# Sixteen stores of rounded weight halves: issued from SyncE's queue or from ScalarE's queue

## The chip, the cores and the metric

The kernel runs on one core of a Trainium2 chip. The metric is the device time of one execution in microseconds (us). Of the kernel before the change there are three timed runs, with a median of 845.52 us (844.38 to 846.73), and one profiled execution, which took 844.22 us and whose profile spans 842.3 us from the first to the last instruction.

## The reference

The work is one attention-like layer followed by a two-layer mixing block, for batch 8, 8 heads, sequence 576 and head size 64 (so the model width is 512 and the hidden width 2048):

```python
kv = np.einsum('bhsd,bhse->bhde', k, v)
out = np.einsum('bhsd,bhde->bhse', q, kv)
rms = np.sqrt(np.mean(out * out, axis=-1, keepdims=True) + 1e-06)
attn = out / rms * g_norm
x = attn.transpose(0, 2, 1, 3).reshape(8, 576, 512)
h = x.transpose(0, 2, 1) @ U @ V            # low rank over the sequence: 576 -> 32 -> 576
u = x + h.transpose(0, 2, 1)
ch = np.maximum(u @ w_ch1, 0.0) @ w_ch2     # 512 -> 2048 -> 512
return u + ch
```

## The kernel before, in words

The two large products, `u @ w_ch1` and the one with `w_ch2`, make up most of the work. TensorE multiplies in a reduced format (`F32R`). To keep float accuracy every operand is split in two: `hi` is the value rounded to `F32R` by a ScalarE cast, and `lo` is the rest, `value - hi`, made by VectorE (`split`, line 143). Each product is then three matmuls: hi by hi, hi by lo, lo by hi.

The 4608 rows of the activation are cut into nine blocks of 512. The first three blocks (`j` = 0, 1, 2; the loop on line 834) are multiplied in the plain way: for each of 16 slices of the hidden width come 12 matmuls of the first layer (`ffn1`, line 511), a rectification with a split on ScalarE (line 524) and VectorE (line 525), and 12 matmuls of the second layer (`ffn2`, line 527). The other six blocks are multiplied in pairs by a scheme of the Strassen-Winograd kind with seven products in place of eight (the loop on line 889). It needs, beside the weights themselves, four sums and differences of the quarters of each weight matrix (`S1` to `S4`). These are the "weight forms".

The forms are made once, during the blocks 1 and 2, by `sums_of_w` (line 259), which is called for 16 pieces: two matrices by eight slices. Each piece has two steps:

- `one` adds the weight halves back together (line 268, two VectorE instructions) and forms the four combinations in place (line 273, four VectorE instructions), in a tile `dec` of 128 by 1024 floats. There are two such tiles, used in turn.
- `two` casts the result to `hi` in the tile `wf` on ScalarE (line 145), subtracts on VectorE so that `dec` holds `lo` (line 146), and stores both to DRAM, as pieces of `w1s` or `w2s`, 512 KB each. There is one `wf` tile (`bufs=1`), so the next piece's cast must wait until the store of `hi` has read `wf`.

The list `PREP` (line 59) gives the place of each piece in the traced order. At the same time the attention of the following batch elements goes on: loads of `kv_sb` and `q_sb`, small matmuls into the banks `pp`, a normalization (lines 358 to 393), a transposition through DRAM (`turn_step`, line 408: stores and loads named `xt`, `ut`), and mixing (`mix_step`, line 496). All its ScalarE and VectorE work shares the two engines with the forms.

Nearly every transfer is issued by SyncE (the rows `SPq`) through the helper `dma` on line 106. One store, on line 662 at the very end, is issued by ScalarE (`ACTq`). Every engine runs its instructions in a fixed order. Which order that is, is settled when the program is built: a planner walks through the traced instructions with a simulated clock and a model of their durations (`schedule_with_timeline_sim=True`, line 961) and puts on each engine what is ready in that simulation. Only instructions given to `keep_in_program_order` are pinned among themselves: nearly all matmuls from line 837 on, the two VectorE additions of line 268, some loads of raw weights and the copies of whole weights to DRAM. The two stores of `two` are not pinned.

Of the kernel before, what the change touches and what calls it, by code (L numbers as in the profile page):

```python
# [10 lines left out]
F32 = mybir.dt.float32  # L11
# [57 lines left out]
def build(ctx: ExitStack, tc: tile.TileContext, kv0_in, kv_in, q_in, uv_in, w_in, out):  # L69
    nc = tc.nc  # L70
# [35 lines left out]
    def dma(out, in_, keep=False):  # L106
        ins = nc.sync.dma_start(out=out, in_=in_)
        if keep:
            tc.keep_in_program_order(ins)
# [5 lines left out]
    def dec_tile(n):  # L115
        return const.tile([P, 2 * DM], F32, name=f"dec{n}", tag=f"dec{n}")
# [26 lines left out]
    def split(hi, lo, src, lo_eng):  # L143

        nc.scalar.copy(out=hi, in_=src)  # L145
        lo_eng.tensor_tensor(out=lo, in0=src, in1=hi.bitcast(F32), op=ALU.subtract)  # L146
# [66 lines left out]
    def halves(t):  # L213
        return t.rearrange("p (a c) -> p a c", a=2)
# [38 lines left out]
    def parts_of_w(which, n):  # L253
        w = "w1 w2".split().index(which)
        return [whole[which, 0] if f == 0 else whole[f][:, 2 * w:2 * w + 2] for f in (n, n + HALF)]
# [3 lines left out]
    def sums_of_w(which, n):  # L259

        c = DM // 2
        t = {}

        def one():
            t["plain"] = a = dec_tile(sets[0] % 2)
            sets[0] += 1
            for k, w in enumerate(parts_of_w(which, n)):
                ins = nc.vector.tensor_tensor(out=halves(a[:, k * DM:(k + 1) * DM]), in0=w[:, :, 0].bitcast(F32), in1=w[:, :, 1].bitcast(F32), op=ALU.add)  # L268
                tc.keep_in_program_order(ins)
            a11, a12, a21, a22 = (a[:, k * c:(k + 1) * c] for k in ((0, 1, 2, 3) if which == "w1" else (0, 2, 1, 3)))  # L270
            for o, in0, in1, op in ((a22, a21, a22, ALU.add), (a21, a11, a21, ALU.subtract), (a11, a22, a11, ALU.subtract),
                                    (a12, a12, a11, ALU.subtract)):
                nc.vector.tensor_tensor(out=o, in0=in0, in1=in1, op=op)  # L273

        def two():
            hi = wf.tile([P, 2 * DM], F32R, name="wf")
            lo = t["plain"].bitcast(F32R)
            split(hi, lo, t["plain"], nc.vector)
            d = dram.tile([P, 4, 2, c], F32, name=f"{which}s{n}")
            for s, part in enumerate((hi, lo)):  # L280
                dma(d[:, :, s], part.bitcast(F32).rearrange("p (a c) -> p a c", a=4))
            for k, name in enumerate(("S2", "S4", "S3", "S1") if which == "w1" else ("S2", "S3", "S4", "S1")):
                wd[which, n, name] = d[:, k]

        return [one, two]
# [684 lines left out]
```

## Time and profile before

| what | value |
|---|---|
| median of three runs | 845.52 us (844.38 to 846.73) |
| profiled execution, its own time | 844.22 us |
| span of its profile | 842.3 us |
| TensorE (PE) busy | 831.6 us, 99% of the span |
| VectorE (DVE) busy | 605.4 us, 72% |
| ScalarE (ACT) busy | 380.0 us, 45% |
| first cast to `wf` for a form / last one | starts at 155.6 / 300.1 us |
| stores of `hi` | 16 of 512 KB, issued by SyncE |
| granted TensorE clock | 1.000 throughout |

A matmul's end is modelled in the profile and matmuls overlap, so the busy time says when TensorE had something running, not how well it ran. What counts for this kernel is the idle time before TensorE's instructions, and what ended it. An idle time of another engine only matters if TensorE ends up waiting behind it.

### The profile page before, as it was taken

How to read it: one execution, taken by the hardware profiler on the slowest of the kernel's cores; microseconds unless marked ns; L12 is line 12 of the kernel's file. 1: busy time of each engine (PE TensorE's matmuls, PEld its weight loads, DVE VectorE, ACT ScalarE, POOL GpSimd, SP SyncE). 2: the span in 40 equal slices, each digit the busy share in tenths (PEclk: the TensorE clock that was granted, in tenths of full speed). 3: DMA queues.
4: the chain of work that ended last, by engine and by line, in shares of the span. 5: the costliest groups of instructions: out<-in, count | busy, mean ns of one | idle time of the engine just before them, and what ended most of it. 6: DMA issues, size and time to landing. Idle time of an engine off the chain costs nothing.

```text
span 842.3 us, 12663 instructions
## 1 busy us (share of the span) xinstructions
PE 831.6 (99%) x4581; PEld 694.3 (82%) x4581; DVE 605.4 (72%) x991; ACT 380.0 (45%) x663; POOL 8.3 (1%) x37
## 2 busy tenths in 40 slices
PE   8999999999999999999999999999999999999998
PEld 8888888888887888888888878888888888888886
DVE  4788655778898877767957898568667965762574
ACT  4766422333244444465436653644355444332431
POOL 3000000000000000000000000000000000000000
PEclk9999999999999999999999999999999999999999
DMA  9996975666487764577878678866765786666665
GB/s 339 385 375 227 370 261 213 237 202 196 139 288 255 222 182 139 162 239 240 258 226 285 208 227 253 273 212 193 228 206 174 224 268 204 184 187 211 193 202 175
DMA packets 105229, 195.00 MB, mean 232 GB/s; under 512 B 10320, under 2 KB 41296, under 8 KB 101456
## 3 DMA queue, kind: packets, MB, share of 16 engines
q1 hardware_dynamic: 105024, 194.07, 70.4%
q8 instruction: 37, 0.61, 0.3%
q14 instruction: 24, 0.20, 0.1%
q10 hardware_dynamic: 144, 0.13, 0.0%
HBM read 142.91 MB, written 51.25 MB: 231 GB/s over the span
## 4 chain that ended last, share of the span: by engine, by line
PE 89%; DVE 5%; DMA 4%; ACT 1%; issue 1%; SPq 0%; DVEq 0%; ACTq 0%
PE y L102 67%; PE h L102 13%; PE pp L102 9%; DMA w2s<-dec 1%; DMA kvq<-kv_in 1%; DMA w2s<-wf 1%; DMA w1s<-wf 1%; DVE dec L268 1%; DVE ss L369 1%; DVE hhl L525 1%; DVE dec L273 1%; ACT wf L145 1%; DMA ringw<-w2s 1%; DVE dec L146 0%; DVE dec L133 0%
## 5 line engine op out<-in xcount | busy, mean ns | idle before, releaser
L102 PE MATMUL y<-entry,ring 128*128 128x512 f32 x576 | 136.0, 390 | 0.0
L102 PE MATMUL y<-hhl,ws 128*128 128x512 f32 x540 | 132.3, 392 | 0.0
L102 PEld LDWEIGHTS y<-entry,ring 128*128 128x128 f32 x576 | 107.5, 188 | 22.2
L102 PE MATMUL h<-uth,ws 128*128 128x512 f32 x360 | 120.4, 395 | 1.4 <-ACT uth L155 0.7
L102 PEld LDWEIGHTS y<-hhl,ws 128*128 128x128 f32 x540 | 99.9, 188 | 20.1
L594 DVE TENSOR_TENSOR h<-y,h 128x512 f32<-128x512 f32 x71 | 48.6, 689 | 57.4 <-PE y L102 52.1
L102 PE MATMUL y<-uB,ringw 128*128 128x512 f32 x354 | 85.0, 391 | 0.0
L638 DVE TENSOR_TENSOR entry<-h,entry 128x1024 fp32r<-128x1024 f32 x48 | 58.6, 1220 | 35.0 <-ACT entry L637 34.8
L102 PE MATMUL y<-uT,ring 128*128 128x512 f32 x348 | 82.4, 390 | 0.0
L102 PEld LDWEIGHTS h<-uth,ws 128*128 128x128 f32 x360 | 67.5, 188 | 16.6 <-DVE hhl L525 1.7
L102 PEld LDWEIGHTS y<-uB,ringw 128*128 128x128 f32 x354 | 66.0, 188 | 13.6
L102 PEld LDWEIGHTS y<-uT,ring 128*128 128x128 f32 x348 | 65.0, 188 | 13.6 <-ACT h L601 0.2
L637 ACT CAST entry<-h 128x1024 fp32r<-128x1024 f32 x48 | 50.5, 1052 | 44.7 <-PE y L102 44.2
L102 PE MATMUL h<-utl,ws 128*128 128x512 f32 x180 | 70.3, 391 | 0.0
L524 ACT ACTIVATE hhl<-h 128x512 fp32r<-128x512 f32 x47 | 28.0, 596 | 76.4 <-PE h L102 76.3
L102 PE MATMUL y<-hhl,ringw 128*128 128x512 f32 x216 | 55.2, 390 | 0.5 <-DMA ringw<-w2s 0.5
L102 PE MATMUL y<-entry,ringw 128*128 128x512 f32 x216 | 55.1, 390 | 0.0
L102 PE MATMUL y<-uT,ringw 128*128 128x512 f32 x210 | 51.0, 391 | 0.0
L102 PEld LDWEIGHTS y<-hhl,ringw 128*128 128x128 f32 x216 | 40.4, 188 | 9.5 <-DMA ringw<-w2s 0.9
L102 PEld LDWEIGHTS y<-entry,ringw 128*128 128x128 f32 x216 | 40.3, 188 | 8.3
L525 DVE SCALAR_TENSOR_TENSOR hhl<-h,hhl 128x512 fp32r<-128x512 f32 x47 | 32.1, 682 | 20.5 <-ACT hhl L524 20.3
L102 PEld LDWEIGHTS y<-uT,ringw 128*128 128x128 f32 x210 | 39.1, 188 | 8.2 <-issue 0.2
(200 smaller groups left out, 1185.9 us busy)
## 6 DMA issues: line engine op xcount, KB each, us to landing
ring<-wd SPq DMA_DIRECT2D x69, 256.0 KB, 3.9
kv_sb<-kv_in SPq DMA_DIRECT2D x14, 1216.0 KB, 7.8
ringw<-wd SPq DMA_DIRECT2D x66, 256.0 KB, 3.7
wd<-ws SPq DMA_DIRECT2D x15, 1024.0 KB, 8.7
raw<-w_in SPq DMA_DIRECT2D x30, 511.8 KB, 10.2
ring<-w1s SPq DMA_DIRECT2D x48, 256.0 KB, 3.6
ringw<-w1s SPq DMA_DIRECT2D x48, 256.0 KB, 3.6
ring<-w2s SPq DMA_DIRECT2D x48, 256.0 KB, 3.7
```

The source lines that it names most:

```text
L102: ins = nc.tensor.matmul(*args, **kw)
L145: nc.scalar.copy(out=hi, in_=src)
L268: ins = nc.vector.tensor_tensor(out=halves(a[:, k * DM:(k + 1) * DM]), in0=w[:, :, 0].bitcast(F32), in1=w[:, :, 1].bitcast(F32), op=ALU.add)
L273: nc.vector.tensor_tensor(out=o, in0=in0, in1=in1, op=op)
L369: nc.vector.tensor_reduce(out=ss.rearrange("p (i h) -> p i h", h=2), in_=xv, axis=AX.X, op=ALU.add)
L524: nc.scalar.activation(out=hh, in_=h, func=AF.Relu)
L525: nc.vector.scalar_tensor_tensor(out=hl, in0=h, scalar=0.0, in1=hh.bitcast(F32), op0=ALU.max, op1=ALU.subtract)
L594: nc.vector.tensor_tensor(out=out, in0=in0, in1=in1, op=ALU.add)
L637: nc.scalar.copy(out=hi, in_=src)
L638: nc.vector.tensor_tensor(out=lo, in0=src, in1=hi.bitcast(F32), op=ALU.subtract)
```

## The change

The store of `hi` is issued by ScalarE on its own queue, where before SyncE issued it. The store of `lo` stays with SyncE. Sizes, destinations and data are the same.

```diff
             lo = t["plain"].bitcast(F32R)
             split(hi, lo, t["plain"], nc.vector)
             d = dram.tile([P, 4, 2, c], F32, name=f"{which}s{n}")
-            for s, part in enumerate((hi, lo)):
-                dma(d[:, :, s], part.bitcast(F32).rearrange("p (a c) -> p a c", a=4))
+            for s, (part, queue) in enumerate(((hi, nc.scalar), (lo, nc.sync))):
+                queue.dma_start(out=d[:, :, s], in_=part.bitcast(F32).rearrange("p (a c) -> p a c", a=4))
             for k, name in enumerate(("S2", "S4", "S3", "S1") if which == "w1" else ("S2", "S3", "S4", "S1")):
                 wd[which, n, name] = d[:, k]
```

## The prediction

> **What bounds the kernel now.** I began with the page, then split the span at the first cast into `wf`, at the last store of a form, and where the tail begins, and read TensorE's idle time in each piece.
>
> ```profile
> span 842.3 us, 12663 instructions
> PE 831.6 (99%) x4581; PEld 694.3 (82%) x4581; DVE 605.4 (72%) x991; ACT 380.0 (45%) x663; POOL 8.3 (1%) x37
> ```
> ```profile
> core 0: us, PE busy (x) PEld busy (x) DVE busy (x) ACT busy (x) POOL busy (x), PEclk, DMA share, GB/s
> 0.00:155.60 155.60, 151.72 (x953) 128.53 (x954) 101.61 (x182) 75.89 (x141) 8.33 (x37) 1.00 0.82 310
> 155.60:302.40 146.80, 144.00 (x897) 119.98 (x896) 124.41 (x250) 58.98 (x118) 0.00 (x0) 1.00 0.66 210
> 302.40:640.00 337.60, 337.12 (x1859) 281.48 (x1858) 251.86 (x414) 167.10 (x301) 0.00 (x0) 1.00 0.71 222
> 640.00:842.30 202.30, 198.73 (x877) 164.28 (x875) 127.53 (x150) 78.07 (x104) 0.00 (x0) 1.00 0.65 203
> ```
>
> TensorE is idle for 842.3 - 831.6 = 10.7 us in all. Of that 155.60 - 151.72 = 3.88 us lie before the first moved store, and 3.57 us in the tail, far behind the last one. The stage that the change touches (155.6 to 302.4 us) has 146.80 - 144.00 = 2.80 us of idle TensorE. So even a perfect change to this stage is worth 2.8 us, about 0.33%. In the stage VectorE is busy for 124.41 of 146.80 us (85%) and ScalarE for 58.98 us (40%): VectorE is the tight helper, ScalarE has room on the average. The clock column stays at 1.00, so it plays no part.
>
> TensorE's own waits in 150 to 300 us, and ScalarE's group of the 16 casts:
>
> ```profile
> PE pp L102 <- DVE x L391: 1.0, 1, 1.0
> PE pp L102 <- DVE st L165: 0.8, 2, 0.5
> PE y L102 <- DVE st L538: 0.6, 1, 0.6
> PE h L102 <- DVE hhl L525: 0.3, 1, 0.3
> ```
> ```profile
> L145 ACT CAST wf<-dec 128x1024 fp32r<-128x1024 f32 x16 | 16.8, 1049 | 16.0 <-DVE dec L273 6.3 <-DMA w1s<-wf 5.6 <-DMA w2s<-wf 4.0
> ```
>
> All of TensorE's waits here end on VectorE. ScalarE sat idle for 5.6 + 4.0 = 9.6 us before its casts because the previous store of `hi` had not yet left `wf`. The question is how much of these 9.6 us reaches TensorE through VectorE, and whether the new queue shortens them.
>
> **The change, part by part.**
>
> *SyncE loses 16 issues.* These are the stores themselves, and how long SyncE waited for the casts:
>
> ```profile
> L107 SPq DMA_DIRECT2D w1s<-wf x8: 513/522/603, 156.7 to 271.0; - x8
> L107 SPq DMA_DIRECT2D w2s<-wf x8: 513/524/712, 168.2 to 301.2; - x8
> DMA to landing us min/median/max: 3.2/4.2/10.1
> ```
> ```profile
> SPq L107 <- ACT wf L145: 17.7, 8, 3.7
> ```
>
> That is 16 x 0.52 = 8.4 us of issue time and 17.7 us of waiting. But the next thing of this piece on SyncE is the store of `lo`, which needs the subtraction behind the same cast, so SyncE mostly waits there instead. None of TensorE's waits above names a transfer. I count this part at nothing. What covers it is that SyncE's loads are wanted well after they are issued. Without that cover it would be worth at most the stage's 2.80 us.
>
> *ScalarE gains 16 issues.* Each waits for its own cast to end, and what stands behind it on ScalarE waits too. The trace has one store issued by ScalarE, of 128 KB; beside it is SyncE's own row for the same line, and the slowest comparable issue on SyncE:
>
> ```profile
> L662 ACTq DMA_DIRECT2D out<-st x1: 374/374/374, 839.6 to 839.6; - x1
> L662 SPq DMA_DIRECT2D out<-st x24: 332/338/405, 494.3 to 839.2; - x24
> L107 SPq DMA_DIRECT2D w2s<-dec x8: 513/682/1329, 169.4 to 302.4; - x8
> ```
>
> ScalarE's 374 ns lie within SyncE's 332 to 405 ns, so I take SyncE's 0.52 us for the 512 KB store; the bounds are 0.37 and 1.33 us. Also lost is the overlap with the next instruction. The places with a late TensorE behind them decide. The first is the cast at 188.18 us, with all its followers up to TensorE's 0.31 us wait:
>
> ```profile
> 178.84 1.05 ACT L145 CAST wf<-dec 128x1024 fp32r<-128x1024 f32 x1 [0.63 <-DVE dec L273]
> 179.01 0.35 SPq L107 DMA_DIRECT2D kv_sb<-kv_in  x1
> 179.92 0.71 SPq L107 DMA_DIRECT2D w2s<-wf  x1
> 184.73 0.60 ACT L524 ACTIVATE hhl<-h 128x512 fp32r<-128x512 f32 x1 [4.41 <-PE h L102]
> 188.18 1.05 ACT L145 CAST wf<-dec 128x1024 fp32r<-128x1024 f32 x1 [2.85 <-DMA w2s<-wf]
> 189.13 0.61 ACT L466 ACTIVATE uth<-ut,g_sb 128x384 fp32r<-128x384 f32 x1
> 189.26 1.22 DVE L146 TENSOR_TENSOR dec<-dec,wf 128x1024 fp32r<-128x1024 f32 x1 [3.04 <-ACT wf L145]
> 190.13 0.26 ACT L359 ACTIVATE x<-pp 64x128 f32<-64x128 f32 x1
> 190.93 0.81 DVE L369 TENSOR_REDUCE ss<-x 128x10 f32<-128x640 f32 x1
> 193.86 0.67 DVE L525 SCALAR_TENSOR_TENSOR hhl<-h,hhl 128x512 fp32r<-128x512 f32 x1
> 194.59 0.50 PE L102 MATMUL h<-uth,ws 128*128 128x512 f32 x1 [0.31 <-DVE hhl L525]
> ```
>
> The cast ends at 189.23; with 0.03 us to release the store (179.92 against the end at 178.84 + 1.05 = 179.89) and 0.52 us of issue, the next activation starts at about 189.78 in place of 189.13, 0.65 us later. Line 359 then ends at 190.13 + 0.26 + 0.65 = 191.04, and the reduction that needs it started at 190.93: 0.1 us late. The rest is hidden behind VectorE's own queue. The second place:
>
> ```profile
> 231.86 0.36 SPq L107 DMA_DIRECT2D kv_sb<-kv_in  x1
> 233.50 0.52 SPq L107 DMA_DIRECT2D w1s<-wf  x1
> 239.69 1.05 ACT L145 CAST wf<-dec 128x1024 fp32r<-128x1024 f32 x1 [4.29 <-DMA w1s<-wf]
> 240.65 0.59 ACT L524 ACTIVATE hhl<-h 128x512 fp32r<-128x512 f32 x1
> 241.92 0.68 DVE L525 SCALAR_TENSOR_TENSOR hhl<-h,hhl 128x512 fp32r<-128x512 f32 x1
> 243.99 0.97 PE L102 MATMUL y<-hhl,w2s 128*128 128x512 f32 x3 [0.58 <-DVE st L538]
> ```
>
> Here the activation at 240.65 would end at 240.65 + 0.59 + 0.65 = 241.89, and VectorE took it up at 241.92: just hidden. So ScalarE's 16 issues cost about +0.1 us. At 1.33 us an issue they add 0.81 us at each of the two places, 1.7 us in all; at 0.37 us they cost nothing. I take +0.1.
>
> *The store of `hi` no longer queues behind SyncE's loads.* It leaves no earlier: on SyncE it already left 0.03 us after the cast. But at both places above a load of `kv_sb` (1216 KB) had been issued 0.91 and 1.64 us before on the same queue, and the chain of waits shows what the stores then took:
>
> ```profile
> 179.92 8.16 DMA w2s<-wf
> 233.50 6.09 DMA w1s<-wf
> 255.70 8.92 DMA w2s<-dec
> ```
>
> 8.16 and 6.09 us against a median of 4.2. At the median the casts could go at 185.33 (after the activation of 184.73) and about 237.7, which is 2.8 and 1.9 us earlier; VectorE's idle 3.04 us before line 146 shrinks alike, and TensorE's 0.31 and 0.58 us go: -0.9 us. If the store shares the DMA engines evenly with the load, it still lands later than 4.2 us. Bounds: -0.9 us and 0. I take -0.6, nearer to the first, since half of the gain in landing already covers the 0.31 and most of the 0.58. The third row is a store of `lo`, which stays on SyncE behind another such load; it leads to the waits on lines 391 and 165 (1.8 us), which stay.
>
> [...]
>
> **Sum.** +0.1 - 0.6 + 0 = -0.5 us on the profiled execution's 844.22 us (span 842.3 and 1.9 around it). That execution lies 1.3 us below the median of the runs; carried to the median, 845.52 - 0.5 = 845.0 us. The known unknowns reach from -0.9 to +1.8 us, 844.6 to 847.3. A change of less than 0.3% (2.5 us) can't be told from none.
>
> **The rivals.**
>
> *The store lands no sooner.* Sixteen engines move the same bytes, and the load is ahead with its packets; then only ScalarE's +0.1 us is left: 845.6 us. [...] Against it: nothing in the trace, but 8.16 against 4.2 us looks like waiting in a line. Chance 0.24.
>
> *The planner writes another order.* The two stores aren't pinned, and a different simulated time on ScalarE and SyncE can put other VectorE instructions first, with VectorE 85% busy. Favourably, all 2.8 us of idle TensorE in the stage go: 842.7 us. Unfavourably, as much is added: 848.3 us. For it: all four of TensorE's waits end on VectorE. Against it: the matmuls are pinned, and most late VectorE instructions have slack. Chance 0.26, evenly over that span, so about 0.05 on either side beyond 2.5 us.
>
> *The store stands behind a waiting activation.* Then the change does not do what it says: "behind the cast" holds in the traced order only. If the planner sets a rectification between cast and store, the store waits for TensorE first.
>
> ```profile
> L524 ACT ACTIVATE hhl<-h 128x512 fp32r<-128x512 f32 x21 | 12.5, 596 | 34.5 <-PE h L102 34.4
> ```
>
> The mean idle time before one is 34.5 / 21 = 1.64 us; with its 0.60 us the store leaves 2.2 us late (after the cast at 178.84 it would be 5.4 us, the activation ending at 185.33). `wf` comes free that much later, the next cast and line 146 with it, and at the two places without slack TensorE waits 2 x 2.2 = 4.5 us: 850.0 us, slower. It decides once the store is over 1.3 us late at both places. Against it: SyncE's stores left right after their casts in the same kind of plan. Chance 0.14.
>
> **How the numbers follow.** The forecast, 845.0 us, has 0.36. Slower by over 0.3%: nearly all of the third rival (0.11), 0.05 of the reordering, and 0.03 for a dear issue, 0.19. Faster by over 0.3%: 0.05 of the reordering and 0.02 for scatter, 0.07. No change: 0.74. The range from 843.2 to 848.6 leaves out the best reorderings (0.04) and the third rival with the worst reorderings (0.15).
>
> **What would show it.** Right: ScalarE shows 16 stores of about 0.5 us, each directly behind its cast; `wf` stores behind a `kv_sb` load land in 4 to 6 us; ScalarE's 9.6 us of idle before the casts fall below 5; idle TensorE from 155 to 302 us stays between 1.5 and 3.5 us. Wrong: the landings stay at 6 to 8 us (first rival); TensorE waits for other VectorE lines (second); activations stand between cast and store (third); or TensorE's idle time changes outside this stage, where I expect none.

## The result

| kernel | median | lowest to highest | executions |
|---|---|---|---|
| before | 844.38 us | 842.60 to 846.73 | 7 |
| after | 849.35 us | 847.99 to 853.24 | 7 |

The ratio after to before is 1.0068, with a 95% interval of 1.0054 to 1.0082: the change costs 5.0 us by the two medians and 5.7 us by the ratio, where 845.0 us and no measurable difference had been forecast, and the result lies above the range. The profiled executions took 844.22 us before and 848.63 us after, a difference of 4.4 us.

The head of the page of the kernel after, and its row for the stage that holds the change (same columns as the table of stretches in the prediction):

```profile
span 846.8 us, 12666 instructions
PE 832.6 (98%) x4581; PEld 695.2 (82%) x4581; DVE 605.9 (72%) x991; ACT 380.4 (45%) x663; POOL 8.3 (1%) x37
```
```profile
155.60:302.40 146.80, 142.09 (x844) 118.64 (x843) 122.17 (x244) 56.06 (x110) 0.00 (x0) 0.98 0.65 205
```

TensorE's idle time in the stage rose from 2.80 to 146.80 - 142.09 = 4.71 us, and the granted clock of the stage is now below 1.00, at 0.98. So part of the loss is idle time, and another part is busy time that became longer.

To see where the loss lies, I took instructions that stand in the same place in both kernels as marks. The first is the cast that starts at 178.84 us before; the timeline after has it so:

```profile
179.61 1.05 ACT L145 CAST wf<-dec 128x1024 fp32r<-128x1024 f32 x1 [0.63 <-DVE dec L273]
```

The other two are TensorE's: a second-layer group (256.20 us before, 255.59 after) and a first-layer group (284.04 before, 288.37 after). TensorE in the stretches between the marks, before and then after (columns: us, PE busy and its records, granted clock, DMA share, GB/s):

```profile
core 0: us, PE busy (x), PEclk, DMA share, GB/s
256.20:284.04 27.84, 25.93 (x170) 1.00 0.79 253
155.60:256.20 100.60, 99.72 (x591) 1.00 0.63 204
284.04:842.30 558.26, 554.21 (x2871) 1.00 0.69 213
```
```profile
255.59:288.37 32.78, 28.07 (x170) 0.90 0.67 211
155.60:255.59 99.99, 99.99 (x594) 1.00 0.64 208
288.37:846.80 558.43, 554.39 (x2871) 1.00 0.68 213
```

At the first mark the kernel after is 0.77 us late; that comes from the start, where two profiles of one kernel differ as well (TensorE idle for 5.45 us before 155.60 us in this profile after and for 4.52 us in a second one). From the first mark to the second it gains 1.38 us (0.77 late becomes 0.61 ahead); some half of that is scatter, since a second profile of the kernel before (the eighth experiment) passes this stretch in 76.67 us where the first took 77.36. Between the second and the third, over the same 170 records, it loses 32.78 - 27.84 = 4.94 us. Behind them it loses 0.17 us. The sum, 0.77 - 1.38 + 4.94 + 0.17 = 4.50 us, is the difference of the spans (846.8 - 842.3). So the whole loss of this pair of profiles sits in some 30 us. Of the 4.94 us, 2.80 are added idle time (4.71 against 1.91) and 2.14 are longer busy time (28.07 against 25.93) at the lower clock.

What happened there is seen in the timeline. Before:

```profile
252.62 1.04 ACT L145 CAST wf<-dec 128x1024 fp32r<-128x1024 f32 x1
253.21 0.38 SPq L107 DMA_DIRECT2D q_sb<-q_in  x1
253.68 0.53 SPq L107 DMA_DIRECT2D w2s<-wf  x1
254.30 0.58 SPq L107 DMA_DIRECT2D kv_sb<-kv_in  x1
258.18 1.05 ACT L145 CAST wf<-dec 128x1024 fp32r<-128x1024 f32 x1 [1.18 <-DMA w2s<-wf]
263.33 1.33 PE L102 MATMUL pp<-kvb,q_sb 128*128 128x128 f32 x10
```

After:

```profile
252.85 0.33 SPq L107 DMA_DIRECT2D kv_sb<-kv_in  x1
253.67 1.05 ACT L145 CAST wf<-dec 128x1024 fp32r<-128x1024 f32 x1
254.76 0.52 ACTq L281 DMA_DIRECT2D w2s<-wf  x1
...
264.03 1.04 ACT L145 CAST wf<-dec 128x1024 fp32r<-128x1024 f32 x1 [7.64 <-DMA w2s<-wf]
264.98 0.72 ACT L153 CAST xh<-x 128x640 fp32r<-128x640 f32 x1
265.75 0.69 PE L102 MATMUL pp<-xh,u 128*64 128x128 f32 x4 [3.61 <-ACT xh L153]
267.91 2.44 PE L102 MATMUL pp<-kvb,q_sb 128*128 128x128 f32 x10
```

Before, the load of `kv_sb` (1216 KB) stood behind the store of `hi` (sixth slice of the second matrix) in SyncE's order: the store went as the cast ended, at 253.66 us, and the load 0.62 us behind it. SyncE hardly waited for the cast here (its issue ahead of the store ended at 253.21 + 0.38 = 253.59); what held the load back was its place. After, the store is no longer ahead of it, and the load goes at 252.85. The store also leaves later, because the planner put the cast behind a few small ScalarE instructions (it starts at 253.67 where it started at 252.62). So the load is 1.91 us ahead of the store, and the store, on its own queue, lands late:

```profile
254.76 9.19 DMA w2s<-wf
```

Before it had landed within 4.4 us. `wf` is a single tile, so the next cast waits 7.64 us at the head of ScalarE. Behind that cast, in ScalarE's fixed order, stands the cast of `x` to `xh`, and TensorE waits 3.61 us for it. During this wait, at 264.3 us, the clock falls (TensorE in stretches of 2 us, columns as above):

```profile
264.00:266.00 2.00, 0.25 (x2) 0.58 0.02 5
266.00:268.00 2.00, 1.39 (x10) 0.50 0.87 291
...
270.00:272.00 2.00, 2.00 (x8) 0.72 0.27 41
```

The ten matmuls `pp<-kvb,q_sb` take 2.44 us at a clock of 0.50 where they took 1.33 us.

The rest of the change went as its description says. All 16 stores are on ScalarE's queue (the row has the eight of `w2s`, with the shortest, median and longest issue in ns; those of `w1s` have the same median), and ScalarE's casts waited for 9.9 us on VectorE and 8.8 us on stores:

```profile
L281 ACTq DMA_DIRECT2D w2s<-wf x8: 520/521/539, 168.6 to 305.5; - x8
```
```profile
L145 ACT CAST wf<-dec 128x1024 fp32r<-128x1024 f32 x16 | 16.8, 1050 | 18.7 <-DVE dec L273 9.9 <-DMA w2s<-wf 8.8
```

### The profile page after: what moved, and what is told of

It reads as the page before. It is cut to its first block, busy times and chain, and to the rows that moved or that the text cites. A ratio compares the mean times of both kernels' runs of the same rounds, so it can differ in the third digit from the quotient of the medians.

```text
span 846.8 us, 12666 instructions
## 1 busy us (share of the span) xinstructions
PE 832.6 (98%) x4581; PEld 695.2 (82%) x4581; DVE 605.9 (72%) x991; ACT 380.4 (45%) x663; POOL 8.3 (1%) x37
## 4 chain that ended last, share of the span: by engine, by line
PE 92%; DMA 5%; DVE 1%; ACT 1%; issue 0%; DVEq 0%; SPq 0%; ACTq 0%
PE y L102 68%; PE h L102 14%; PE pp L102 10%; DMA kv_sb<-kv_in 1%; DMA kvq<-q_in 1%; DMA w2s<-wf 1%; DMA raw<-w_in 1%; DMA uvs<-uv_in 1%; DVE dec L133 0%; ACT wf L145 0%; DVE st L165 0%; DVE hhl L525 0%; DVE ws L146 0%; DVE dec L146 0%; DVE dec L268 0%
```

## The experiments

The theory, A, is: the loss is one load overtaking one store. SyncE, which no longer has the `hi` store ahead of the `kv_sb` load, issues the load first; the store lands late, the next cast waits, the cast of `xh` waits behind it, TensorE stands idle and loses its clock. The rivals are: ScalarE's own queue is at fault, whatever stands ahead of it; the 16 issues load ScalarE; the planner's exchanged instructions cost the time.

**Take the load away, leave the change.** One `kv_sb` load of the kernel after is put one place later in the traced order (67 for 66); all 16 stores stay on ScalarE.

```diff
-            at(base + steps[name], what)
+            at(base + steps[name] + (1 if (name, b, p) == ("kvl", 3, 2) else 0), what)
```

> The changed kernel with one load of kv_sb traced one place later (place 67 in place of 66), so that on SyncE it stands behind both stores of this pair of forms; ScalarE's and VectorE's orders are those of the changed kernel. Theory A (one place: the store of hi at 254.8 us runs beside a kv_sb load that left 1.9 us before it, lands after 9.2 us, holds the next cast 7.6 us and with it TensorE 3.6 us, whose clock then drops): the store lands in 3 to 5 us, TensorE's wait on xh is gone, the granted clock stays at 1.00, and the time is 842.5 to 844.5 us, 0 to 2 us below before. Theory B (sixteen issues on ScalarE and two queues at work cost a little everywhere): still 848 to 850 us. Theory C (the new order on VectorE and ScalarE is at fault, whatever the load does): still 847 to 850 us.

Measured: 843.53 us (841.64 to 846.66, 10 executions) against 843.26 us for the kernel before beside it, ratio 1.0007 (0.9994 to 1.0020). The timeline, and the stage's row:

```profile
254.48 0.52 ACTq L281 DMA_DIRECT2D w2s<-wf  x1
...
258.07 1.05 ACT L145 CAST wf<-dec 128x1024 fp32r<-128x1024 f32 x1 [1.97 <-DVE dec L273]
...
264.65 0.45 SPq L107 DMA_DIRECT2D kv_sb<-kv_in  x1
```
```profile
155.60:302.40 146.80, 145.93 (x909) 122.19 (x908) 127.23 (x257) 60.64 (x120) 0.00 (x0) 1.00 0.67 214
```

With the load out of the way (it now goes at 264.65) the store lands in 3.2 us, the next cast waits for VectorE alone, the wait on `xh` is gone, and the clock stays at 1.00. Idle TensorE in the stage is 146.80 - 145.93 = 0.87 us. Against the kernel before as it stood, the measured loss is gone with one load's place. That doesn't yet say that nothing else was lost: the load's later place also helps the kernel before (the seventh and tenth experiments), and against that kernel this one is 0.2 to 0.3% slower.

**Give only that store back to SyncE.** In the kernel after, the one store goes back to SyncE; the other 15 stay with ScalarE.

```diff
-for s, (part, queue) in enumerate(((hi, nc.scalar), (lo, nc.sync))):
+for s, (part, queue) in enumerate(((hi, nc.sync if (which, n) == ("w2", 5) else nc.scalar), (lo, nc.sync))):
```

> The changed kernel with the store of hi of that one piece (w2, slice 5) back on SyncE, where it now stands behind the kv_sb load; the other 15 stay on ScalarE, and all other orders are the same. Theory A: not the queue but the load ahead of it is the cause, so the store lands in 7 to 10 us again and the time stays at 847 to 850 us. Theory A2 (a queue of its own loses against the load's larger packets; in the load's own queue it would be faster): lands in 4 to 6 us, 843 to 845 us. Theory B: one issue of 16 is gone, 849 us.

Measured: 848.39 us (846.95 to 848.93), ratio 1.0058 (1.0041 to 1.0075). The planner left the load ahead of the store, now in one queue:

```profile
252.38 0.33 SPq L107 DMA_DIRECT2D kv_sb<-kv_in  x1
...
254.30 0.53 SPq L281 DMA_DIRECT2D w2s<-wf  x1
...
262.23 1.05 ACT L145 CAST wf<-dec 128x1024 fp32r<-128x1024 f32 x1 [6.30 <-DMA w2s<-wf]
```
```profile
254.30 7.83 DMA w2s<-wf
```

The store is on SyncE's queue and nearly the whole loss stays. So it is not ScalarE's queue as such; the place behind the load is enough. Behind the load in one queue the store landed after 7.83 us; on its own queue beside the load it took 7.3 to 9.2 us in four profiles, so no difference between the queues can be read from this.

**Make only that store's change.** In the kernel before, this one store goes to ScalarE; the other 15 stay with SyncE. VectorE's order is that of the kernel before.

```diff
-for s, part in enumerate((hi, lo)):
-    dma(d[:, :, s], part.bitcast(F32).rearrange("p (a c) -> p a c", a=4))
+for s, (part, queue) in enumerate(((hi, nc.scalar if (which, n) == ("w2", 5) else nc.sync), (lo, nc.sync))):
+    queue.dma_start(out=d[:, :, s], in_=part.bitcast(F32).rearrange("p (a c) -> p a c", a=4))
```

> The kernel before with the store of hi of this one piece alone on ScalarE; VectorE's order is that of before, ScalarE's too but for one exchange of two small instructions. On SyncE the kv_sb load is no longer held up behind the store's wait and leaves before it. Theory A: the store lands in 6 to 9 us instead of 4.4, the next cast and the xh cast behind it come 2 to 4 us late, and the time rises by 2 to 5 us to 846.5 to 849.5 us, nearly all of the change's loss with a sixteenth of it. Theory B: +0.3 us. Theory C: no new order, 844 to 845 us.

Measured: 848.09 us (846.91 to 851.84), ratio 1.0065 (1.0040 to 1.0091).

```profile
253.57 0.33 SPq L107 DMA_DIRECT2D kv_sb<-kv_in  x1
253.80 0.59 ACTq L281 DMA_DIRECT2D w2s<-wf  x1
...
262.14 1.05 ACT L145 CAST wf<-dec 128x1024 fp32r<-128x1024 f32 x1 [5.03 <-DMA w2s<-wf]
...
263.87 0.46 PE L102 MATMUL pp<-xh,u 128*64 128x128 f32 x4 [1.63 <-ACT xh L153]
266.28 0.27 PE L102 MATMUL pp<-xh,u 128*64 128x128 f32 x1 [1.95 <-DVE xh L404]
```

A sixteenth of the change makes the whole loss, without 15 of the issues, without an exchange on VectorE, and with the cast in its old place on ScalarE (one pair of small ScalarE instructions is exchanged behind it). The load leads by only 0.23 us, and the store still takes 262.10 - 253.80 = 8.3 us to land.

**Move the late cast, first try.** In the kernel after, entry 12 of `PREP`, counted from zero, which is the piece behind the late store, is put two places later (68 for 66), so that the cast of `xh` comes ahead of the waiting cast.

```diff
-PREP = [37, 37, 41, 43, 47, 49, 53, 57, 56, 63, 63, 66, 66, 69, 75, 78]
+PREP = [37, 37, 41, 43, 47, 49, 53, 57, 56, 63, 63, 66, 68, 69, 75, 78]
```

> The changed kernel with the next piece's second step (cast, subtraction, stores) two places later (68 for 66 in PREP), so that on ScalarE the xh cast stands before the cast that waits for wf. All 16 stores stay on ScalarE and the kv_sb load stays early. Theory A: the store still lands in 7 to 10 us, but nobody TensorE needs stands behind it; TensorE's wait on xh is gone and the time is 842 to 845 us. Theory B: still 848 to 850 us. Theory C: VectorE's order is new again, so anything from 843 to 850 us.

Measured: 847.02 us (845.50 to 851.75), ratio 1.0052 (1.0030 to 1.0074), span of the profile 844.2 us, clock 1.00. The wait on `xh` is gone. But the piece's VectorE work now lies elsewhere, and TensorE waits there, from 250 us on (total, times and longest in us):

```profile
PE pp L102 <- DVE t L447: 1.7, 2, 1.5
PE h L102 <- DVE hhl L525: 0.9, 1, 0.9
```

So A's 842 to 845 us were missed, and most of the loss stayed; the waits that the profile shows lie behind VectorE. A further wait of 1.06 us, at 195 us, lies far ahead of the moved piece, behind a store that took 8.9 us to land. A's 7 to 10 us for the late store were missed too: the planner moved its cast as well, the store left 2.9 us behind the load, and it landed in 4.9 us. That another order on VectorE can cost this much is the prediction's second rival; here the edit brought it about, and the run tells little of A's first links.

**Fill TensorE's wait.** In the kernel after, ten matmuls of 128x512, whose results are overwritten, are set ahead of the matmuls that wait for `xh`. They are added work; nothing is left out.

```diff
-        todo = [(xh, i) for i in range(NT)] + [(xl, i) for i in range(4)]
+        todo = [(xh, i) for i in range(NT)] + [(xl, i) for i in range(4)]; [mm(tp, lhsT=w1s[4][0][0], rhs=ut[2][0][:, 0, :], start=True, stop=True) for _ in range(10 if (b, p) == (3, 1) else 0)]
```

> The changed kernel with ten more matmuls of 128x512 put on TensorE just before those that wait for xh at 262 us; their result is overwritten by the matmuls behind them. They are extra work of some 10 x 0.227 = 2.3 us, all inside the wait of 3.6 us. Theory A with the clock (the wait costs its own length and then again, since the granted clock falls to 0.5 for some 6 us behind it): the wait left is about 1.3 us, the granted clock stays at 1.00, and in spite of the added work the time falls by 2 to 3 us, to 845 to 847 us. Theory A without the clock (the fall of the clock costs nothing that isn't hidden): the time stays at 848 to 849 us, or rises.

Measured: 847.61 us (844.56 to 850.92, 10 executions), ratio 1.0039 (1.0017 to 1.0061). The profiled execution was the longest of the ten, 850.92 us. Two stretches of it, at the filled place and later:

```profile
266.00:268.00 2.00, 2.00 (x13) 1.00 0.64 192
...
490.00:520.00 30.00, 26.92 (x115) 0.89 0.62 183
```
```profile
505.26 1.65 PE L102 MATMUL y<-hhl,ringw 128*128 128x512 f32 x3 [3.08 <-DMA ringw<-w2s]
```

At the filled place the clock stays at 1.00, where it fell to 0.50 in the kernel after, though the cast still waits 6.04 us for the store: the fall of the clock at this place came from TensorE's idleness. But this execution met another wait of 3.08 us, on a ring load at 505 us, with another fall of the clock, and the median missed the expected 845 to 847 us. The mean clock of each execution tells the two cases apart: six of the ten had 0.999 or 1.000, with a median of 845.6 us, and four 0.996 to 0.998, with 849.4 us. Of the unfilled kernel, all seven executions had 0.996 or 0.998. The longer busy time above (2.14 us) remains the direct size of the clock's part.

**Move the late cast, second try.** Only the second step of that piece (cast, subtraction and stores) goes four places later; the load stays early.

```diff
-            at(PREP[k] + m, what)
+            at(PREP[k] + m + (4 if (k, m) == (12, 1) else 0), what)
```

> The changed kernel with the second step of the next piece (w1, slice 6) traced four places later, its first step left where it is: on ScalarE its cast, which waits for wf, then stands well behind the xh cast. The kv_sb load still leaves before the store at 254.8 us. Theory A: that store lands after 7 to 10 us as in the changed kernel, but no instruction that TensorE needs stands behind a cast that waits for it; the wait on xh is gone, the granted clock stays at 1.00, the time is 842.5 to 845.5 us, unless the shifted cast makes VectorE late elsewhere, which the trace would show. Theory A' (the load's traffic itself, not ScalarE's order, delays xh): still 847 to 850 us.

Measured: 845.14 us (843.82 to 847.64, 10 executions), ratio 1.0018 (1.0003 to 1.0034), clock 1.00.

```profile
252.73 0.33 SPq L107 DMA_DIRECT2D kv_sb<-kv_in  x1
...
259.02 0.73 ACT L153 CAST xh<-x 128x640 fp32r<-128x640 f32 x1 [2.75 <-DVE x L393]
...
276.25 1.39 PE L102 MATMUL pp<-kv_sb 128*64 128x64 f32 x40 [1.59 <-DVE t L447]
```

The load still leads the store, but nothing that TensorE wants stands behind the waiting cast. About three quarters of the loss are gone (from 0.68% to 0.18%). The profile shows a new wait of 1.59 us behind VectorE, made by the moved step; with 146.80 - 143.90 = 2.90 us the stage's idle time is near that of the kernel before, so where the rest of the 0.18% lies is not shown. So the middle link of A, the cast of `xh` in line behind the cast of `wf`, is shown too.

**The same move in the kernel before.** The load goes one place later, with all stores on SyncE.

```diff
-            at(base + steps[name], what)
+            at(base + steps[name] + (1 if (name, b, p) == ("kvl", 3, 2) else 0), what)
```

> The kernel before, all stores on SyncE, with the same one load of kv_sb traced a place later as in the first experiment; ScalarE's and VectorE's orders are those of before. Theory A says that the queue of the 16 stores in itself is worth nothing, so this and the first experiment (842.5 to 844.5 us expected there, 843.5 measured) agree within 1 us: 842 to 844 us. If ScalarE's queue had a gain of its own of the predicted 0.5 to 1 us, this one would be the slower by so much.

Measured: 842.02 us (840.47 to 843.47, 10 executions), ratio 0.9974 (0.9960 to 0.9988).

```profile
155.60:302.40 146.80, 145.58 (x907) 121.95 (x906) 126.79 (x257) 59.99 (x120) 0.00 (x0) 1.00 0.67 214
```

Theory A expected this run within 1 us of the first experiment (843.53 us); it is 1.5 us faster. Idle TensorE in the stage is 1.22 us, and TensorE's wait of 1.0 us on line 391 is gone. In the kernel before, the load stood ahead of the `lo` store of the same piece, which landed after 8.92 us (a row in the prediction); now that takes 3.3 us.

**The kernel before, profiled once more.**

> The kernel before, unchanged, for a second profile of it. All theories: the same orders, a time of 842 to 847 us; idle TensorE from 155.6 to 302.4 us within 1 us of the first profile's 2.80 us, which tells how far two profiles of one kernel differ.

One execution took 843.17 us, with 2.20 us of idle TensorE in the stage, against 2.80 in the first profile. Differences of half a microsecond between single profiles mean nothing here. One number of the prediction is such a difference: the store at 180 us, which took 8.16 us to land in the first profile, took 6.4 us in this one, on the same queue and in the same order, and the wait of 0.31 us at 194 us is gone.

**Both late-load kernels again, on one chip.** The two are the first and the seventh experiment, unchanged.

> The changed kernel with the one kv_sb load a place later, a second time, beside the next run on the same chip; its first profile was of its fastest execution. If the whole loss is the overtaking load, then without it ScalarE's queue costs nothing and this kernel lies within 0.1% of the next run: both near 0.9975 of before. If ScalarE's 16 issues and the exchanged places cost something by themselves, it lies 1 to 2.5 us above the next run, near 1.000 of before, and its profile shows one or more waits of TensorE that the next run's lacks, on VectorE or on a store, at 155 to 302 us or in the stage behind it.

> The kernel before with the same load a place later, a second time, to see whether its lead was that one call's: 842.0 us and 0.996 to 0.999 of before if it is real; within 0.999 to 1.001 if it was the chip's spread. Idle TensorE at 155.6 to 302.4 us below 2.2 us.

Measured: with ScalarE's stores 844.16 us (842.10 to 848.88, 12 executions), ratio 1.0008 (0.9992 to 1.0025); with SyncE's stores 842.47 us (840.66 to 845.10, 12 executions), ratio 0.9988 (0.9978 to 0.9999). The rank repeats: the late load makes the kernel before faster, by 0.26% and 0.12%, and with ScalarE's stores the median is 1.5 and 1.7 us higher. By the median this is the second of the two outcomes named ahead of the ninth experiment, that something beside the overtaking load costs time. But the intervals of the second pair overlap, and the profiled spans don't show the gap (839.8 and 840.8 us with ScalarE's stores, 840.2 and 840.6 without). Among the executions with a mean clock of 0.999 or more the second gap is gone (medians of 842.56 and 842.47 us), and the first is 1.15 us. The second profile with ScalarE's stores has a wait that may belong to it:

```profile
PE y L102 <- DMA ringw<-w2s: 1.1, 1, 1.1
```

**The kernel after, profiled once more.**

> The changed kernel unchanged, one more profile: near 848.5 us, the store of the eleventh piece's hi landing after 8 to 10 us behind the early kv_sb load, ScalarE's cast waiting 6 to 8 us for it, TensorE waiting over 2 us on the cast of x behind it, and the clock at 0.5 there. If that place were chance of one execution, the wait would be gone or elsewhere.

One execution, 850.12 us:

```profile
252.74 0.33 SPq L107 DMA_DIRECT2D kv_sb<-kv_in  x1
...
263.51 1.04 ACT L145 CAST wf<-dec 128x1024 fp32r<-128x1024 f32 x1 [7.23 <-DMA w2s<-wf]
```

The same place, the load again early, nearly the same wait. It isn't chance of one execution. Between the same two marks of TensorE this profile takes 33.36 us (255.48 to 288.84) and the second profile of the kernel before 27.55 us (255.63 to 283.18): a loss of 5.81 us, against 4.94 in the first pair.

## Why the prediction was wrong

**The step that failed: "SyncE loses 16 issues ... I count this part at nothing."** The reasoning looked at SyncE's 17.7 us of waiting as lost or not lost time, and found that SyncE would wait for the store of `lo` instead, and that its loads are wanted well after they are issued. Both miss the order: at one place the `kv_sb` load stood between the two stores, behind that of `hi`. With this store gone from SyncE's order the load went at 252.85 instead of 254.30 us, ahead of the store, which landed in 9.2 us instead of 4.4. It cost 4.94 us over the 170 matmul records behind it. The bound given for this part, at most a gain of 2.80 us, had no loss side at all, and so the range ended too low. The load's lateness was not a cost that could be saved; it protected the store.

**ScalarE's issues.** Each took 0.52 us, as taken over from SyncE's row. The +0.1 us expected at 188 us can't be seen: TensorE's wait behind that place is in none of the profiles with ScalarE's stores but the fourth experiment's, where the store ahead of it landed in 8.9 us.

**"The store of `hi` no longer queues behind SyncE's loads": not borne out at the two places, reversed at a third.** At the two places the prediction named, the store stood behind a load before and after. Timeline of the two casts that follow, after:

```profile
187.19 1.05 ACT L145 CAST wf<-dec 128x1024 fp32r<-128x1024 f32 x1 [1.16 <-DMA w2s<-wf]
...
239.42 1.05 ACT L145 CAST wf<-dec 128x1024 fp32r<-128x1024 f32 x1 [3.87 <-DVE dec L273]
```

The first store left at 180.68 and landed in 6.4 us (8.16 before), the second took 5.6 us (6.09 before). This pair of profiles alone suggests a gain; all of them together don't. With these stores on SyncE's queue, five profiles have 8.2, 6.4, 6.8, 6.4 and 7.2 us at the first place and 5.7 to 6.1 at the second; on ScalarE's queue, eight have 6.4 to 6.8 and once 8.9 at the first and 5.6 to 5.9 at the second. So the 8.16 us, on which most of the term of -0.6 us rested, was the chance of one profile.

TensorE's idle time from 155.60 us to the second mark did go from 0.88 us to 0. Of that, the 0.31 us show in only one of the five profiles with SyncE's stores; the wait at 243 us is in all five (0.20 to 0.58 us) and in none of the eight others, but there the planner also exchanged two VectorE instructions (line 538 now stands ahead of line 369), so what the queue has to do with it is not shown. At the third place, which had no `kv_sb` load ahead of the store before and so was not looked at, landing went from 4.4 to 9.2 us.

That a store on a queue of its own lands sooner behind a load that left before it, from which the -0.6 us comes, was the author's estimate, and no run shows the term. In the profile after, with the store on ScalarE's queue and the load on SyncE's, the store landed behind the load at all three places: 187.1 us against 185.8, 239.3 against 237.9 and 264.0 against 261.5. At the third place a queue of its own gave 7.3 to 9.2 us and a place behind the load in one queue 7.83 us.

**The rivals.** The store that lands no sooner was right about the two places; its 845.6 us failed for the third. The planner's other order was real but not needed for the loss: the third experiment has it without an exchange on VectorE. The store behind a waiting activation named 850.0 us, close to the 849.35 measured, but by a mechanism that did not occur (no store left more than 0.15 us after its cast); a fitting number is no sign of a fitting cause. Its structure (a late `wf`, a late cast, TensorE waiting) was right, with another reason for the lateness: not a late issue, but a slow landing.

**The sums.** The 845.52 us to which the forecast was carried came from three executions; seven have a median of 844.38. The upper bound of +1.8 us counts the 0.1 us of the first place twice (2 x 0.81 + 0.1 = 1.7). By its own even spread over 5.6 us the reordering has 0.26 x 0.3 / 5.6 = 0.01 on either side beyond 2.5 us, not 0.05. None of this would have put 849 us inside the range.

**"What would show it."** Stores of about 0.5 us on ScalarE: right. `wf` stores behind a load landing in 4 to 6 us: only about (6.4 and 5.6, then 9.2). ScalarE's idle time before casts, for stores, below 5 us: wrong, 8.8 us, of it 7.64 at the one place. Idle TensorE of 1.5 to 3.5 us: wrong, 4.71 us. The sentence that the clock "plays no part" held for the profile before and was carried over to the kernel after, where 2.14 us of the loss hang on it.

**What stays open.** With the overtaking load removed, ScalarE's stores still had a median 1.5 to 1.7 us above SyncE's, so 0.2 to 0.3% of the change's 0.7% may have another cause; against that, one store alone made the whole loss in the third experiment. The profiles don't settle whether the rest is the queue, the exchanged instructions, or waits and falls of the clock that only some executions have. A candidate is the ring load at about 500 us: TensorE waits 0.68 to 3.08 us for it in four of the eight profiles with ScalarE's stores, and at most 0.5 us in the five others. Why the store lands late when the load leaves first is also only described by the runs: they show the order and the times, not the cause.

## What to carry to other kernels

A place in an in-order queue is also an order: when an instruction is moved off a queue, list what stands behind it there, ask how much sooner each will now go, and which transfers it will then be ahead of: here a load went 1.45 us sooner, 1.91 us ahead of a store that then took 9.2 us to land instead of 4.4. Where a single-buffered tile is written by an engine with a fixed order, a late transfer also holds what stands behind the waiting instruction (here the cast waited 7.64 us for the store, and TensorE 3.61 us for the cast of `xh` behind it), so look at what stands there and not only at the tile's own users. Here the better edit was to the load: put one place later in the kernel before, it gave 842.02 and 842.47 us in two measurements (ratios 0.9974 and 0.9988), below both kernels.

## What the runs showed of the hardware

**A queue of its own did not protect a store from a load that left shortly before it.** With the 1216 KB load 1.9 us ahead, the 512 KB store took 7.3 to 9.2 us to land from ScalarE's queue (four profiles: 9.2, 8.8, 7.6 and 7.3), and 7.8 us from SyncE's, behind the load in one queue (one profile). A lead of 0.23 us gave 8.3 us, and one of 2.9 us (the fourth experiment) 4.9. With the load 0.6 us behind the store it took 4.4 and 4.3 us, both on SyncE's queue. With the load out of the way it took 3.2 us from ScalarE's queue (twice) and 3.5 and 4.0 us from SyncE's. At the two places at 180 and 233 us, where the load leads by 0.9 and 1.6 us on either queue, the queues differ by no more than two profiles of one kernel do: at 180 us the store took 6.4 to 8.2 us from SyncE's queue and 6.4 to 8.9 from ScalarE's, at 233 us 5.7 to 6.1 and 5.6 to 5.9, and the two profiles of the kernel before have 8.16 and 6.4 us at the first.

**The clock fell for 3.4 or 6.8 us at a time, and not by the length of one wait.** In the kernel after it was at 0.50 from 264.3 to 271.1 us, though TensorE worked again from 265.75, after a wait of 3.61 us. With the store back on SyncE the longest wait was 2.31 us (TensorE's share in two stretches there):

```profile
264.00:268.00 4.00, 3.26 (x18) 0.52 0.84 278
266.00:270.00 4.00, 4.00 (x17) 0.50 0.59 164
```

In stretches of half a microsecond the fall lasts 6.8 us here too, and in the second profile of the kernel after (265.9 to 272.8 us); in the third experiment, after two waits of 1.63 and 1.95 us within 4 us, it lasts 3.4 us (266.4 to 269.9). A single wait of 1.59 us (the sixth experiment) left the clock at 1.00. But no limit for one wait can be read from this: in the kernel after the clock fell 2.2 us into the wait, in its second profile 0.7 us after a wait of 3.23 us had ended, and in the tenth experiment it fell at 32.9 us, for 3.4 us (mean clock 0.99 up to 155.60 us), with TensorE shown as busy for all of the 6 us before.
